# Two query tiles and two token tiles per step in a four-layer attention kernel

## The chip, the cores and the metric

The kernel runs on one core of a Trainium2 chip. The time is the device time of one execution in microseconds; the runs of the kernel before are summarised by their median. One further execution was recorded by the hardware profiler; its engine rows are the profile. The engines are PE (TensorE, matrix products into PSUM), ACT (ScalarE), DVE (VectorE), POOL (GpSimd) and SP (SyncE, which here only issues DMAs). PEld is the loading of a stationary operand into PE.

## The reference

The input is one sequence of 2048 tokens with 512 features, in bf16. Four residual layers follow each other: A, B, A, B, with the same weights for both A and both B:

```
x = x + A(layernorm(x));  x = x + B(layernorm(x));  and both once more

A: q, k, v = x wq, x wk, x wv           32 heads of 16, 4 segments of 512 tokens
   for each segment s:
     p      = softmax(q_s k_s^T / 4 + causal mask within the segment)
     a_dot  = p v_s
     a_mem  = phi(q_s) M / (phi(q_s) z + 1e-6)      phi(t) = t + 1 if t > 0 else exp(t)
     o_s    = g a_mem + (1 - g) a_dot               g = sigmoid(beta), per head
     M, z  += phi(k_s)^T v_s, sum of phi(k_s)
   return o wo

B: q, k, v = x wqkv;  pq, pk = q w_phi, k w_phi (16x16 per head)
   phi_q = [softmax(pq), softmax(-pq)], phi_k the same
   kv = phi_k^T v, z = sum of phi_k  over all 2048 tokens
   return (phi_q kv / (phi_q z + 1e-6)) wo
```

A works on segments of 512 tokens. B needs the sums over all tokens before its first query can be finished.

## The kernel before

Tokens are cut into 16 tiles of 128, four to a segment; heads into four groups of eight, a group being 128 of the 512 features. The residual X stays on chip for all four layers. `build` (L1035) runs through the layers L = 0 and 1 (each one A and one B): in A for each segment `a_proj` (K, Q, V and the memory sums), then `a_att` for each query tile, `out_proj` and the next layer's norm (`ln`) for each pair of tiles, then B's `b_keys` for the segment; after the fourth segment `b_query` for each of the four segments, in the first pass together with the norm and the projections of the second A.

Each function only writes down operations: an engine or a choice of engines, what it reads and writes, and which buffer it opens. The order of all operations is a written-out table (`ORDER`, L1106 on): `place` (L157) unpacks from it the order of the 3047 operations, the engine of each, and the buffer of each tile. `emit` hands each engine its operations in that order, with the waits on semaphores that the data and the reuse of buffers need. An engine thus never overtakes within its own list, SP and POOL neither.

The buffers that matter: PSUM is cut into four tiles D of 128 x 1024 fp32 (two banks each), used in turn for projections, scores, value products and outputs. `p1` are 20 buffers of 128 x 512, `p2` 18 of 128 x 1024, `pE` four for masked probabilities.

Where a matrix product has 64 rows, two of them run side by side, one in each half of PE's rows, and write the two banks of one D. `pair` (L330) splits a projection in that way into two operations of eight matmuls; both banks are complete after the second.

`a_att(L, s, i)` (L759) takes one query tile i of a segment. For each group of heads and each key tile j up to i it forms scores in a D (128 keys in rows, 1024 columns: eight heads by 128 queries) with eight matmuls of 128 columns (label S). On the diagonal, j = i, keys and queries are halved and the empty quarter is left out, 768 columns, and two matmuls with `two64` and `tri` add the mask (Sd). One ACT instruction takes the exponential (L351, 1024 elements a row, or 768 into a `pE` buffer). Then the value products (PV, L326): 16 matmuls of 34 columns for each key tile, probabilities stationary, values with a column of ones moving; all four groups of a tile collect in one D. When the four groups are there, DVE takes for each half of the heads the reciprocals (`rden`, 16 columns, L389) and the product (`pvn`, 256 elements, L834), adds the memory part (`oadd`, L842), and a DMA on SP (or PE for the last tile) transposes the tile for the output projection.

`out_proj` (L864) multiplies by wo for two tiles at once, but adds to X tile by tile: on DVE (`res`, 512 elements, L879), or, for certain tiles of B, X is added on PE and the sum evacuated (L359 on ACT or L360 on DVE). In the second B each tile is stored by its own DMA (issued through L368).

`a_proj` evacuates K, Q and V from PSUM by `evac`, on ACT (L359) or DVE (L360) as the table says, V tile by tile with 512 elements. `b_keys` (L903) projects keys and values for two tiles at once, but takes the exponentials (+ and -, L351) and their sums over 16 features (L925) tile by tile with 512 elements. Tiles 14 and 15 are projected singly.

## Time and profile before

| | |
|---|---|
| Runs of the kernel before | 494.85, 496.53, 498.26 us, median 496.53 |
| The profiled execution | 492.6 us, of which 490.9 us from the first to the last instruction (the span) |
| Instructions | 27,235: PE 12,490 matmuls and as many weight loads, DVE 1087, ACT 605, POOL 144 |
| Exponentials and other ACT work | 256 of 1024 elements, 128 of 768, 112 of 512, 55 evacuations, 54 small ones |
| Chain that ended last, by engine | PE 59%, ACT 25%, DVE 8%, issue 3%, DMA 3% |
| HBM read and written | 6.32 and 2.10 MB |

A group row names a line of the kernel, the engine, the operation, what it writes and reads, the shapes, and a count; then the busy time in us, the mean of one in ns, and the idle time ahead of the group with what ended it. Consecutive instructions of one engine overlap in these rows, the next begins before the last has left; a step is the distance of their starts. Line 326 is all of PE's work written by `mm`, 341 all written by `pair`, 351 all of ACT's written by `act`.

A row of the chain is the start in us, a length, and who was at work. A row of the windows is a stretch in us and its length; then for PE, PEld, DVE, ACT and POOL the busy time with the number of instructions; then the clock granted to PE as a share of the full one, the DMA engines' busy share and the GB/s. On the page each digit is the busy tenth of one of 40 slices of 12.3 us.

### The profile page before, as it was taken

Reading aid. Unit: us, or ns where it says so; the run is one execution under the profiler, and the core shown is the slowest. Engines: PE = TensorE matmul, PEld = TensorE weight load, DVE = VectorE, ACT = ScalarE, POOL = GpSimd, SP = SyncE. Lnnn points to the kernel's source line nnn. Section 1 sums busy time; section 2 is a strip of 40 time slices with the busy share of each in tenths; the row PEclk is TensorE's granted clock in tenths of the full one; section 3 lists DMA queues with packets and bytes.
Section 4 is the critical chain, followed back from the end, with each engine's and each line's share of the span. In section 5 each row is a group of like instructions: output and inputs, shape, how many; then the busy total and the mean of one; then the engine's idle time right before and its main releaser. Section 6 shows DMA issues by size and latency. Waiting matters only on the chain.

```text
span 490.9 us, 27235 instructions
## 1 busy us (share of the span) xinstructions
PE 460.2 (94%) x12490; PEld 309.1 (63%) x12490; DVE 436.1 (89%) x1087; ACT 433.9 (88%) x605; POOL 59.6 (12%) x144
## 2 busy tenths in 40 slices
PE   7899999999999989999999999899999999998896
PEld 3457666576667666665656766576577676665553
DVE  6899899899989969888999999899989997998884
ACT  3799899999999889579999999899999999858882
POOL 4701031010011001000230240100010010100000
PEclk9999999999999999999999999999999999999599
DMA  8761554441315021001124445153304133200255
GB/s 233 203 117 37 80 107 66 90 70 32 41 38 73 5 54 28 13 3 24 27 55 79 90 57 90 15 79 60 68 4 57 26 44 38 47 3 3 51 109 169
DMA packets 89459, 30.50 MB, mean 62 GB/s; under 512 B 76000, under 2 KB 89344, under 8 KB 89344
## 3 DMA queue, kind: packets, MB, share of 16 engines
q1 hardware_dynamic: 88992, 28.46, 31.7%
q8 instruction: 98, 1.61, 1.4%
q10 hardware_dynamic: 288, 0.26, 0.2%
q14 instruction: 17, 0.14, 0.1%
q0 software_dynamic: 64, 0.02, 0.1%
HBM read 6.32 MB, written 2.10 MB: 17 GB/s over the span
## 4 chain that ended last, share of the span: by engine, by line
PE 59%; ACT 25%; DVE 8%; issue 3%; DMA 3%; SPq 1%; POOL 0%; POOLq 0%; DVEq 0%
PE D L341 36%; PE D L326 21%; ACT p L351 16%; ACT pE L351 6%; DMA WA_q<-in_A_wq_dram 2%; DVE pQ L672 1%; ACT pS L351 1%; DVE p L756 1%; DVE pS L925 1%; PE D L854 1%; DVE pK L360 1%; ACT pV L359 1%; DVE p L591 1%; ACT p L359 1%; DVE p L360 1%
## 5 line engine op out<-in xcount | busy, mean ns | idle before, releaser
L351 ACT ACTIVATE p<-D 128x1024 bf16<-128x1024 f32 (+1 forms) x368 | 312.1, 913 | 25.2 <-PE D L326 11.6
L326 PE MATMUL D<-pK,pQ 64*128 64x128 bf16 (+1 forms) x2560 | 115.5, 211 | 4.3 <-ACT p L351 1.4
L326 PEld LDWEIGHTS D<-pK,pQ 64*128 64x128 bf16 x2560 | 80.7, 94 | 43.4 <-ACT p L351 10.9
L351 ACT ACTIVATE pE<-D 128x768 bf16<-128x768 f32 x128 | 102.0, 835 | 4.7 <-PE D L326 3.6
L326 PE MATMUL D<-pV,p 64*128 64x34 bf16 x1536 | 73.4, 176 | 3.9 <-issue 2.9
L326 PE MATMUL D<-pV,pE 64*128 64x34 bf16 x1024 | 75.2, 175 | 0.5 <-ACT pE L351 0.2
L326 PE MATMUL D<-pW,pE 64*128 64x34 bf16 x1024 | 73.0, 175 | 0.1
L326 PE MATMUL D<-pW,p 64*128 64x34 bf16 x1536 | 71.7, 176 | 1.0 <-issue 0.9
L326 PEld LDWEIGHTS D<-pV,p 64*128 64x128 bf16 x1536 | 66.8, 93 | 7.1 <-issue 2.4
L326 PEld LDWEIGHTS D<-pW,p 64*128 64x128 bf16 x1536 | 65.8, 93 | 3.9 <-issue 1.4
L341 PE MATMUL D<-pX,WA_k 64*128 64x512 bf16 x256 | 65.2, 376 | 2.1 <-DMA WA_q<-in_A_wq_dram 1.4
L341 PE MATMUL D<-pX,WA_q 64*128 64x512 bf16 x256 | 65.3, 377 | 0.6 <-issue 0.4
L578 POOL TENSOR_SCALAR rstd<-mv 128x1 f32<-128x1 f32 x60 | 14.9, 265 | 374.0 <-DVE mv L571 367.2
L326 PEld LDWEIGHTS D<-pV,pE 64*128 64x128 bf16 x1024 | 54.8, 93 | 3.1 <-issue 1.5
L326 PEld LDWEIGHTS D<-pW,pE 64*128 64x128 bf16 x1024 | 51.2, 93 | 0.9 <-issue 0.3
L570 DVE BATCH_NORM_STATS2 stats<-X 128x6 f32<-128x512 bf16 x64 | 42.5, 681 | 4.7 <-DMA X<-in_A_x_dram 4.6
L925 DVE TENSOR_REDUCE pS<-p 128x32 f32<-128x512 bf16 x64 | 42.1, 672 | 2.1 <-ACT p L351 1.9
L672 DVE TENSOR_SCALAR pQ<-p,m 128x512 bf16<-128x512 bf16 x128 | 42.6, 355 | 0.6 <-ACT p L359 0.5
L879 DVE TENSOR_TENSOR X<-X,D 128x512 bf16<-128x512 bf16 x48 | 31.1, 682 | 7.3 <-PE D L341 7.1
L580 POOL TENSOR_TENSOR rstd<-rstd,mhalf 128x1 f32<-128x1 f32 x60 | 36.4, 624 | 2.8
L341 PE MATMUL D<-WA_o,p 64*128 64x512 bf16 (+1 forms) x288 | 33.8, 353 | 2.3 <-issue 1.9
L326 PE MATMUL D<-tri,two 64*128 64x256 bf16 x256 | 35.2, 270 | 0.0
(117 smaller groups left out, 848.9 us busy)
## 6 DMA issues: line engine op xcount, KB each, us to landing
pW<-pV SPq DMA_DIRECT2D x16, 136.0 KB, 2.7
out_dram<-X SPq DMA_DIRECT2D x16, 128.0 KB, 1.9
X<-in_A_x_dram SPq DMA_DIRECT2D x3, 512.0 KB, 7.5
pX<-in_B_wqkv_dram SPq DMA_DIRECT2D x3, 512.0 KB, 5.4
p<-p SPq DMA_TRANSPOSE x76, 3.2
pX<-p SPq DMA_TRANSPOSE x54, 3.2
WA_k<-in_A_wk_dram SPq DMA_DIRECT2D x2, 256.0 KB, 6.7
WA_v<-in_A_wv_dram SPq DMA_DIRECT2D x1, 512.0 KB, 8.0
```

Of the source, the lines that this page charges most:

```text
L326: ins = e.matmul(out_ap, lhsT, rhs, start=st, stop=sp, tile_position=(basep(lhsT), basep(out_ap)))
L341: ins = e.matmul(out_ap, lhsT[64 * hf:64 * hf + 64], rhs[64 * hf:64 * hf + 64], start=k == 0 and i == 0, stop=k == 1 and i == len(lists[hf ...
L351: return self.g.op({"act": (dur, lambda e: e.activation(out_ap(), in_ap(), func, scale=scale))}, reads, writes, opens, label=label)
L359: ch = {"act": (n / 1.2 + 51, lambda e: e.activation(out_ap(), in_ap(), ACT.Copy)), "dve": ((340 if fast else n / 0.96 + 65), lambda e: e. ...
L360: "dve": ((340 if fast else n / 0.96 + 65), lambda e: e.tensor_copy(out_ap(), in_ap()))}
L570: v(lambda e: e.bn_stats(self.stats[:, t, :], self.X[:, t, :]), 602, [R("X", t)], [R("st", t)], label="bn")
L578: v(lambda e: e.tensor_scalar(rs, self.mv[:, t, 1:2], LN_EPS, None, op0=ALU.add), 170, [R("mv", t)], [R("rstd", t)], eng="pool", label="rstd")
L580: v(lambda e: e.tensor_tensor(rs, rs, self.mhalf[:], ALU.pow), 540, [R("rstd", t), R("mhalf")], [R("rstd", t)], eng="pool", label="rstd")
L591: v(lambda e: e.tensor_scalar(xn.t[:], self.X[:, t, :], self.mv[:, t, 0:1], self.rstd[:, t:t + 1], op0=ALU.subtract, op1=ALU.mult), 300, [ ...
L672: fn = lambda e, KM=KM, KT=KT, sl=sl: e.tensor_scalar(KM.t[:, :, sl % 2, :, 64 * (sl // 2):64 * (sl // 2) + 64], KT.t[:].rearrange("p (j h ...
L879: self.v(lambda e, X=X, src=src: e.tensor_tensor(X(), X(), src(), ALU.add), 602, [R("X", t), ps[512 * k]], [R("X", t)], label="res")
L925: fn = lambda e, sgn=sgn, E=E, Z=Z: e.tensor_reduce(Z.t[:, sgn * 32:(sgn + 1) * 32], E.t[:, sgn * 512:(sgn + 1) * 512].rearrange("p (h d) ...
```

## The change

Layer A takes two query tiles i0 and i0 + 1 together. Scores against the key tiles before them are formed for 256 queries and half of the heads of a group in a D (four matmuls of 256 columns). Against key tile i0 both query tiles have scores, and only the first one's are on the diagonal: a new form `Sf`, 896 elements a row, with its own buffers `pF`. Against key tile i0 + 1 only the second has, in the old diagonal form. Value products collect in a D for two groups of heads and both tiles, so that each reciprocal, product and addition works on half of the features of both tiles. That reorders the features of o, so the rows of wo are loaded in another order, in four DMAs instead of one, and the memory part is written in the new order too. o and its transpose are 128 x 1024 in `p2`.

Values are evacuated two tiles at a time, residual sums and stores too, and the exponentials of B's keys and their sums. `p1` has 16 buffers instead of 20, `p2` 19 instead of 18, `pE` two instead of four, `pF` three.

The table is new. It lists 2912 operations: PE 1054 (1022 before), ACT 566 (606), DVE 964 (1087), POOL 140 (140), SP 188 (192). Matmuls are not operations here; one operation of PE issues several.

```diff
-        ldw(lambda: self.WA["o"], inp["A_wo"], R("WA", "o"))
+        for kk in range(4):
+            load(lambda kk=kk: [(self.WA["o"][:, kk, :], inp["A_wo"].rearrange("(g k a x) o -> g a k x o", g=2, k=4, a=2)[kk // 2, kk % 2])], 128, [R("WA", "o", kk)])
...
-            for k in range(2):
-                self.evac(lambda tt=t2 + k: VT.t[:, tt, :, 0:16], ..., 512, [ps[k * 512]], [VT[t2 + k]], label="Vev")
+            self.evac(lambda t2=t2: VT.t[:, t2:t2 + 2, :, 0:16]..., 1024, [ps[0], ps[512]], [VT[t2], VT[t2 + 1]], label="Vev")
...
-    def a_att(self, L, s, i):
+    def a_att(self, L, s, i0):
...
+        for gg in range(2):
+            PV = self.T(self.pD, "pv")
+            for g in (2 * gg, 2 * gg + 1):
...
+                for j in range(i0 + 1):
+                    for p in range(2):
+                        S = self.T(self.pD, "S")
+                        if j < i0:
+                            P = PT[(p, j)] = self.T(self.p2, "PT")
+                            self.mm(lambda ...: [(S.t[:, hf * 512 + x * 256:hf * 512 + x * 256 + 256], key(hf, j, p, x), qry(hf, 0, 256), True, True)
+                                                 for x in range(2) for hf in range(2)], [], rd, [S], opens=[P], label="S", rows=64, dur=222)
+                            self.act(lambda P=P: P.t[:], lambda S=S: S.t[:], ACT.Exp, 1024, [S], [P], scale=0.25, label="exp")
+                        else:
+                            P = PF[p] = self.T(self.pF, "PF")
+                            self.mm(lambda ...: [
+                                (S.t[:, hf * 512 + 256 - 192 * x:hf * 512 + 512 - 256 * x], key(hf, j, p, x), qry(hf, 64 * x, 256 - 64 * x), x == 0, False)
+                                for x in range(2) for hf in range(2)] + [... two(hf), tri(hf, 2), False, True) for hf in range(2)],
+                                [], rd + trir, [S], opens=[P], label="Sf", rows=64, dur=252)
+                            self.act(lambda P=P: P.t[:, :, 64:512], lambda S=S: ...[:, :, 64:512], ACT.Exp, 896, [S], [P],
+                                     scale=0.25, label="expf")
...
+            v(lambda e, pvv=pvv, rden=rden: self.recip(e, rden(), pvv()[:, :, :, 16]), self.dur_recip(32), pvr, [Rt], label="rden")
+            v(lambda e, ...: e.tensor_tensor(part(o)..., pvv()[:, :, :, 0:16], rden()..., ALU.mult), 598, pvr + [Rt], [o[gg]], label="pvn")
+            if s >= 1:
+                v(lambda e, part=part: e.tensor_tensor(part(o), part(o), part(tmp), ALU.add), 335, [o[gg], tmp], [o[gg]], label="oadd", port=True)
...
+                self.tr(dst, lambda part=part: part(o), [o[gg]], [oT[gg]], [oT] if gg == 0 else [], label="otr")
...
-        for k, t in enumerate(ts):
...
+            self.v(lambda e: e.tensor_tensor(X(), X(), src(), ALU.add), 65 + 512 * n / 0.96, pr + xr, xr, label="res")
+        if store:
+            self.dma(lambda: [(self.out[0][t0 * 128:(t0 + n) * 128, :].rearrange("(t p) d -> p t d", p=128), self.X[:, t0:t0 + n, :])], 1, xr, [], lat=1900.0, label="store")
...
+                for sgn in range(2):
...
+                    self.act(..., ACT.Exp, 512 * n, [S[0], S[512]][:n], [E[sgn]], scale=1.0 - 2.0 * sgn, label="kexp")
...
+                    v(fn, 65 + 512 * n / 0.96, [E[sgn]], [Z[sgn]], label="Zred")
...
-                for i in range(4):
+                for i0 in (0, 2):
...
-N_XT, N_KM, N_K1, N_K2, N_VT, N_SM, N_QT, N_PE = 5, 6, 20, 18, 5, 6, 6, 4
+N_XT, N_KM, N_K1, N_K2, N_VT, N_SM, N_QT, N_PE, N_PF = 5, 6, 16, 19, 5, 6, 6, 2, 3
```

## The prediction

> **What bounds the kernel now.** I read the page's busy shares and slices first, then the chain of waits, then the groups by shape, then the timeline at the two ends.

> ```profile
> PE 460.2 (94%) x12490; PEld 309.1 (63%) x12490; DVE 436.1 (89%) x1087; ACT 433.9 (88%) x605; POOL 59.6 (12%) x144
> ...
> PE   7899999999999989999999999899999999998896
> ...
> DVE  6899899899989969888999999899989997998884
> ACT  3799899999999889579999999899999999858882
> ...
> PEclk9999999999999999999999999999999999999599
> ```

> Three engines are nearly full from slice 2 to slice 34; none alone is the limit. PE's 94% contains modelled ends: its columns, N/2.4 ns each with the two row halves side by side (a pair of 34-column value products starts every 25 ns in the timeline), come to 414 us, 84%. What keeps the others from 100% is mostly the start (ACT 3, 7) and the last five slices. In the two attention stretches, 40-200 and 217-425 us, the windows give ACT 347.8 us busy of 368, DVE 334.2, PE 349.8. Inside them the chain is ACT back to back, with PE's projections between:

> ```profile
> 362.57 0.92 ACT p L351
> 363.49 0.70 ACT pE L351
> 364.20 0.92 ACT p L351
> 365.11 0.70 ACT pE L351
> ...
> 373.92 0.50 ACT p L351
> ```

> These are the steps that one instruction really takes in a full queue: 1024 elements 0.917 us, 768 0.704, 512 0.49, so 0.833 ns per element and 0.063 fixed (the groups' means, 1043, 835 and 616 ns, contain the overlap with the next). DVE likewise, first in the timeline, then in the groups by shape:

> ```profile
> 265.45 1.29 DVE L360 CAST pV<-D 128x512 bf16<-128x512 f32 x2
> ```

> ```profile
> L925 DVE TENSOR_REDUCE pS<-p 128x32 f32<-128x512 bf16 x64 | 42.1, 672 | 2.1 <-ACT p L351 1.9
> L879 DVE TENSOR_TENSOR X<-X,D 128x512 bf16<-128x512 bf16 x48 | 31.1, 682 | 7.3 <-PE D L341 7.1
> ...
> L834 DVE TENSOR_TENSOR p<-D,pS 128x256 bf16<-128x256 f32 x64 | 25.3, 417 | 0.3
> ...
> L389 DVE RECIPROCAL pS<-D 128x16 f32<-128x16 f32 x64 | 13.4, 235 | 9.1 <-PE D L326 8.8
> ```

> Two casts in 1.29, one alone 0.69: a step of 0.60 for 512 elements, 0.533 for the elements and 0.067 fixed. So joining two operations saves 0.063 on ACT and 0.067 on DVE, and nothing else.

> **The change, engine by engine.** Assignments are those of the new order table, unpacked as the kernel unpacks it.

> PE. For one layer, segment and group, the scores were 6 full tiles (8 matmuls) and 4 diagonal ones (10), 88 matmuls; now 4 full (4), 4 half-masked (6), 2 diagonal (10): 60. Columns per row half: 6x512 + 4x640 = 5632 before, 4x512 + 4x576 + 2x640 = 5632 after. The same columns in half the matmuls stand side by side in the trace:

> ```profile
> 262.04 0.60 PE L341 MATMUL D<-WB_o,p 64*128 64x256 bf16 x8
> ...
> 262.48 0.61 PE L326 MATMUL D<-pK,pQ 64*128 64x128 bf16 x16
> ```

> 1024 columns a half take 0.60 as 8 and 0.61 as 16: at most 0.01 us for 8 matmuls fewer, so the 896 that go are worth 0 to -1.1 us. Value products stay at 5120, every projection stays. PE: 414.3 to 414.2.

> ACT. Score exponentials: 192x0.917 + 128x0.704 = 266.2; after, 128x0.917 + 128 of 896 elements + 64x0.704. No row has 896; between 768 and 1024 the ends are 0.704 and 0.917, which is 13.6 us either way over 128; the three measured sizes lie on a line within 10 ns, so I take 0.810 and get 266.2, no change, +-1.3. Key exponentials: 64x0.49 = 31.4 to 28x0.917 + 8x0.49 = 29.6 (-1.8). Value evacuations on ACT: 8x0.49 to 3x0.917 (-1.2). K and Q evacuations: 21 to 16 (-2.5). Weight folding: 3x0.49 + 1.07 to none (-2.5). Residual evacuations: 9x0.49 to 5x0.917 + 2x0.49 (+1.2). One each more of four small ones (+2.1). Sum -4.7: 419.6 to 414.9.

> [...]

> DVE. Products with the reciprocals: 64x0.334 to 32x0.60 (-2.2). Reciprocals: 64 of 16 columns to 32 of 32; the rows for 32 and 64 columns (334, 536 ns) give 6.3 ns a column, so each pair saves its fixed part, 0.03 to 0.067; I take 0.06 (-1.9). Key sums 64x0.60 to 28x1.133 + 8x0.60 (-1.9). Residual sums 48x0.60 to 22x1.133 + 4x0.60 (-1.5). Residual evacuations 7x0.60 to 1.133 + 2x0.60 (-1.9). Values 24x0.60 to 13x1.133 (+0.3). K, Q, folds, taken over from ACT (+5.4). Small ones -1.2. Sum -4.9: 422.4 to 417.5. The memory product keeps its 12x1024 elements in a longer pattern; L756 and L950, differently strided, both take 1.22, so 0. The 24 additions keep their size.

> Sums of 415-418 on three engines for a span of 491 mean that the order decides. The saved ACT time lies in the stretches where ACT is 94% busy; DVE has the same saving, so it does not become late in its place. PE is next: by columns it is 88% full there, and 4.7 us in 368 makes it 89%. Of the -4.7 I take -3.5; the ends are -5.6 (idle time shrinking in proportion, 4.7x491/415 = 5.6) and 0.

> **Start.** PE's first projection waits for weights:

> ```profile
> 3.30 8.56 DMA WA_q<-in_A_wq_dram
> ```

> Ahead of and with it went 2048 KB (four X tiles, half of wk, X 4-7, wv, half of wq). In the new table two of the four wo quarters (256 KB) stand second and fourth on SP, but wv and one half are behind: 1792 KB. At the 215 GB/s of the first 10 us, 256 KB are 1.2 us. Against it X tile 2 is issued one place later (0.5 us; PE's transposes end at 10.5 now, 1.4 before the weights). SP's seventh issue took 2.96 us in before, the others about half a microsecond; now the seventh is a weight half. Ends -1.2 and +1, taken -0.7.

> **End.** Sixteen stores become nine.

> ```profile
> 485.88 3.12 SPq L368 DMA_DIRECT2D out_dram<-X  x6
> ```

> The chain's last piece, a cast of 0.69 us at 486.39, gives the last result at 487.1, but SP still issues until 489.0, and landing takes 1.9. With pairs the queue is empty sooner; the last paired sum (1.13 instead of 0.60) takes part of it back. Ends -1.3 and 0, taken -0.8.

> **Waits and queues.** The two halves of a projected pair both end with its second set of eight matmuls, before and after, so a joined evacuation, exponential or residual sum waits for nothing new; it gives the first tile's half 0.53 us later (1.13 against 0.60), and behind it on DVE stands that tile's norm, 0.6 us a tile, whose consumer is a 3.2 us DMA. I cost this at 0 where other tiles' work is queued, which is everywhere but at the last pair. SP's transposes keep their number (110 of o and x, 28 others) and size. POOL has seven small memsets for six, and one of its four gate products is DVE's now (in the small ones above). A transposed half of o now holds both tiles, so the first tile of a pair waits for the second: rival 2.

> Sum: -3.5 - 0.7 - 0.8 = -5.0, from 492.6 to 487.6 in the profiled execution (span 490.9 and 1.7 around it). The three runs shown have a median of 496.5, so I put the forecast there: 491.5.

> **Rivals.**

> 1. The saving falls into idle time. In the list of waits ACT waits for PE 40 us in all, PE's weight loads for ACT 25; if the new order only widens these, the two ends remain: -1.5 at best, 495 to 497. For it: DVE and ACT save by almost the same amount while PE saves nothing. Against it: 94% ACT in 368 us.

> 2. The hand-over from A to B gets longer, and the kernel slower. Tiles 14 and 15 used to end one after the other, tile 14's projection, norm and transposing DMA (3.2 us) beneath tile 15's scores; now both end with the last pair. Summed by steps over the order, the work between the last value product of layer A and the first denominators of B grows from PE 18.1 and DVE 19.1 us to 26.0 and 28.6 in the second half of the kernel, and from 18.1 and 23.3 to 25.0 and 28.8 in the first, while ACT has 16 to 19. Cut at the last value product of each segment, at these points and where B of the first layer gives way to A of the second (its first scores, its last projection), the busiest engine's sums come to 436.0 before and 440.3 after: +4.3, in the ratio of 491 to 448 (the sum with 12 us of start) +4.7: 501, with start and end at nothing. It decides if the earlier stretches do not shorten by what moved: the first three segments go from 129.3 to 128.4 only.

> 3. The clock.

> ```profile
> 450.00:455.00 5.00, 3.30 (x194) 2.77 (x194) 3.35 (x12) 4.80 (x11) 0.00 (x0) 0.98 0.01 3
> 455.00:460.00 5.00, 3.50 (x136) 2.94 (x130) 4.26 (x10) 4.79 (x11) 0.00 (x0) 0.50 0.11 24
> 460.00:465.00 5.00, 4.82 (x54) 2.67 (x56) 3.81 (x10) 4.33 (x7) 0.00 (x0) 0.50 0.43 74
> ```

> PE, two thirds busy at 450-460, runs at 0.50 until 465: eight matmuls of a projection that take 1.04 took 1.89 at 460, about 3 us lost. The same place in the first half kept 1.00. If the longer hand-over leaves PE idle there too, +3; if the stretch goes, -3. [...] Alone: 494 to 500.

> **Numbers.** Forecast 0.48, rival 1 0.22, rival 2 0.22, rival 3 alone 0.08. A measurement of this kernel tells about 1% from no change: below 491.6 is faster, above 501.5 slower. Of the forecast's chance 0.38 lies below, rival 3's better side adds 0.02; rival 1 and the rest of the forecast are within; rival 2 and 3 together reach 504. Faster 0.40, same 0.34, slower 0.26. Range: below, -5.6 - 1.2 - 1.3 - 3 = -11.1, 485; above, +4.7 + 3 = +7.7, 504.

> **What would show it.** ACT near 429 us busy with 565 instructions, DVE near 431 with 964, PE's matmuls 11,594; the 896-element exponential at about 940 ns mean; first projection near 11.2; last result within 3 us of the end. Wrong would be: ACT under 90% in the attention stretches, more than 22 us between the last value product and the first denominators, or a second 5 in the clock's row.

## Result, and the profile after

The changed kernel takes 482.92 us (median; 481.20 to 483.33), the kernel before on the same chip 497.39 (494.85 to 498.28): a ratio of 0.971, 95% interval 0.967 to 0.976, some 14 us less. The forecast was 491.5. The profiled execution took 483.33 us with a span of 481.6. Medians, here and below, take in every execution of a kernel; ratios leave out those that took over 1.5% longer than its fastest.

The page of the kernel after, its engine sums and its slices:

```profile
PE 455.0 (94%) x11594; PEld 298.9 (62%) x11594; DVE 436.1 (91%) x964; ACT 426.9 (89%) x565; POOL 60.1 (12%) x144
...
PE   7889899989999999998999999999999989999896
...
DVE  4999999989899998988999999999999987998893
ACT  3499999999999997488999999999999999586992
...
PEclk9999999999999999998999999999999999999798
```

The counts are those of the prediction, and ACT lost 7.0 us of busy time. DVE lost 123 instructions and no busy time, PE 5.2 us. So the engines' work explains at most half of the 14 us. The groups by shape of the kernel after (busy time and mean, then the idle time ahead and what ended it):

```profile
L351 ACT ACTIVATE pF<-D 128x896 bf16<-128x896 f32 x128 | 117.6, 949 | 2.5 <-PE D L326 2.0
L942 DVE TENSOR_REDUCE pS<-p 128x64 f32<-128x1024 bf16 x28 | 33.4, 1208 | 1.6 <-ACT p L351 1.6
L895 DVE TENSOR_TENSOR X<-X,D 128x1024 bf16<-128x1024 bf16 x22 | 26.7, 1219 | 7.6 <-PE D L341 7.2
L844 DVE TENSOR_TENSOR p<-D,pS 128x512 bf16<-128x512 f32 x32 | 21.9, 685 | 0.5
L389 DVE RECIPROCAL pS<-D 128x32 f32<-128x32 f32 x32 | 11.3, 353 | 2.4 <-PE D L326 2.1
```

The joined forms cost what was worked out. What is new stands in the last column: DVE's reciprocals waited 9.1 us for PE's value products before and wait 2.4 now. PE became earlier there, though it has the same columns to multiply. The rest of the study is about why.

**A place where PE stands still.** Two rows of the groups of before were there to be read and were not:

```profile
L326 PE MATMUL D<-pV,p 64*128 64x34 bf16 x1536 | 73.4, 176 | 3.9 <-issue 2.9
...
L326 PE MATMUL D<-pW,p 64*128 64x34 bf16 x1536 | 71.7, 176 | 1.0 <-issue 0.9
```

"Issue" is idle time that no semaphore ended. These matmuls lie inside an operation of 16; what the operation waits for, its first matmul has waited for. To find where the idle time lies, PE's recorded instructions (a weight load, a matmul and a recorded wait each count as one) were numbered from the first, and the idle time was sorted by the number modulo 256, in 64 places of four. One place stands out: 192 to 195, with 7.2 of the 25.1 us that PE is idle in the kernel before. The other 63 places have about 0.3 us each. The queue q8, which carries instructions, counts blocks of the same size. Before:

```profile
q8 instruction: 98, 1.61, 1.4%
```

After:

```profile
q8 instruction: 91, 1.49, 1.3%
```

```profile
PE D L326 <- issue: 8.6, 15, 1.2
...
PE D L341 <- issue: 2.5, 4, 1.0
```

The kernel after:

```profile
PE D L341 <- issue: 1.3, 1, 1.3
...
PE D L326 <- issue: 1.0, 3, 0.5
```

All kernels of the study, "place" being PE's idle time at the border, in us, in the profiled execution. Ratios are against the kernel before on the same chip:

```
kernel                          median  ratio [95%]            span   place  matmuls
before, first profile           497.39  -                      490.9   7.2   12,490
before, profiled again          499.63  -                      497.8  13.1   12,490
  same order, token joins       501.63  1.004 [1.000, 1.008]   499.6  11.6   12,490
  +64 small matmuls             507.64  1.020 [1.012, 1.028]   504.2  18.0   12,554
  +128                          500.21  0.999 [0.995, 1.002]   498.6  11.3   12,618
  value products, full rows     501.38  1.002 [0.999, 1.006]   500.4   1.2    9,930
after                           482.92  0.971 [0.967, 0.976]   481.6   1.4   11,594
  +32 small matmuls             493.06  0.985 [0.982, 0.989]   490.9  11.0   11,626
  +64                           500.32  1.001 [0.997, 1.005]   498.6  16.1   11,658
  +128                          483.78  0.967 [0.964, 0.971]   482.0   1.1   11,722
  full scores in 128 columns    496.16  0.994 [0.990, 0.998]   496.3  14.0   12,106
  all scores in 128 columns     503.46  1.008 [1.005, 1.012]   502.9  19.8   12,618
  value products, full rows     496.65  0.996 [0.992, 0.999]   495.0   1.5    9,034
  token joins undone            487.30  0.974 [0.968, 0.980]   485.2   1.6   11,594
  division joins undone         488.07  0.976 [0.970, 0.981]   485.8   1.8   11,594
  all joins undone              492.28  0.985 [0.982, 0.988]   489.5   2.0   11,594
  other load order              483.10  0.968 [0.961, 0.976]   484.3   2.6   11,594
  load order, 173 cuts          482.50  0.963 [0.961, 0.966]   481.7   2.0   11,767
  2048 instructions of waits    562.55  1.129 [1.122, 1.135]   563.3   6.9   11,594
```

### The profile page after: what moved, and what is told of

The parts are those of the page before. It is cut to its first block, busy times and chain, and to the rows that moved or that the text cites. A ratio compares the mean times of both kernels' runs of the same rounds, so it can differ in the third digit from the quotient of the medians.

```text
span 481.6 us, 25267 instructions
## 1 busy us (share of the span) xinstructions
PE 455.0 (94%) x11594; PEld 298.9 (62%) x11594; DVE 436.1 (91%) x964; ACT 426.9 (89%) x565; POOL 60.1 (12%) x144
## 4 chain that ended last, share of the span: by engine, by line
PE 59%; ACT 26%; DVE 7%; DMA 3%; issue 2%; POOL 1%; SPq 0%; DVEq 0%
PE D L341 38%; PE D L326 20%; ACT p L351 13%; ACT pF L351 9%; ACT pE L351 3%; DMA p<-p 2%; DVE pQ L676 1%; DMA X<-in_A_x_dram 1%; DVE stats L574 1%; POOL rstd L584 1%; ACT pS L351 1%; PE D L864 1%; DVE p L595 1%; DVE X L895 1%; DVE p L761 1%
## 5 line engine op out<-in xcount | busy, mean ns | idle before, releaser
L351 ACT ACTIVATE p<-D 128x1024 bf16<-128x1024 f32 (+1 forms) x276 | 251.6, 964 | 27.2 <-PE D L341 19.5
L326 PE MATMUL D<-pK,pQ 64*128 64x256 bf16 (+3 forms) x1536 | 114.8, 243 | 7.1 <-ACT p L351 2.3
L351 ACT ACTIVATE pF<-D 128x896 bf16<-128x896 f32 x128 | 117.6, 949 | 2.5 <-PE D L326 2.0
L326 PEld LDWEIGHTS D<-pK,pQ 64*128 64x128 bf16 x1536 | 54.7, 94 | 45.7 <-ACT pF L351 6.9
L326 PE MATMUL D<-pV,pF 64*128 64x34 bf16 x1024 | 76.4, 176 | 2.4 <-ACT pF L351 1.1
L326 PE MATMUL D<-pW,pF 64*128 64x34 bf16 x1024 | 74.3, 176 | 0.0
L341 PE MATMUL D<-pX,WA_k 64*128 64x512 bf16 x256 | 64.7, 376 | 0.9 <-ACT pX L359 0.8
L341 PE MATMUL D<-pX,WA_q 64*128 64x512 bf16 x256 | 64.7, 377 | 0.0
L326 PEld LDWEIGHTS D<-pV,pF 64*128 64x128 bf16 x1024 | 56.9, 93 | 5.7 <-ACT pF L351 2.3
L351 ACT ACTIVATE pE<-D 128x768 bf16<-128x768 f32 x64 | 53.1, 839 | 1.8 <-PE D L326 1.2
L326 PEld LDWEIGHTS D<-pW,pF 64*128 64x128 bf16 x1024 | 53.5, 93 | 1.1
L326 PE MATMUL D<-pV,p 64*128 64x34 bf16 x1024 | 52.2, 176 | 0.1
L326 PE MATMUL D<-pW,p 64*128 64x34 bf16 x1024 | 51.3, 176 | 0.0
L326 PEld LDWEIGHTS D<-pV,p 64*128 64x128 bf16 x1024 | 46.8, 93 | 2.5 <-ACT pF L351 0.4
L326 PEld LDWEIGHTS D<-pW,p 64*128 64x128 bf16 x1024 | 45.5, 93 | 1.5
L326 PE MATMUL D<-tri,two 64*128 64x128 bf16 (+1 forms) x384 | 45.9, 234 | 0.0
L326 PE MATMUL D<-pV,pE 64*128 64x34 bf16 x512 | 44.7, 175 | 0.0
L326 PE MATMUL D<-pW,pE 64*128 64x34 bf16 x512 | 42.9, 175 | 0.4 <-issue 0.2
L942 DVE TENSOR_REDUCE pS<-p 128x64 f32<-128x1024 bf16 (+1 forms) x36 | 38.3, 1086 | 1.6 <-ACT p L351 1.6
```

Of the source, the lines that this page charges most:

```text
L326: ins = e.matmul(out_ap, lhsT, rhs, start=st, stop=sp, tile_position=(basep(lhsT), basep(out_ap)))
L341: ins = e.matmul(out_ap, lhsT[64 * hf:64 * hf + 64], rhs[64 * hf:64 * hf + 64], start=k == 0 and i == 0, stop=k == 1 and i == len(lists[hf ...
L351: return self.g.op({"act": (dur, lambda e: e.activation(out_ap(), in_ap(), func, scale=scale))}, reads, writes, opens, label=label)
L942: fn = lambda e, sgn=sgn, eo=eo, Z=Z, n=n: e.tensor_reduce(Z.t[:, 0:64 * n].rearrange("p (k s h) -> p k s h", k=n, s=2)[:, :, sgn, :], eo( ...
```

## Experiments

**First group: joins against PE's program.** If the time came from fewer and larger instructions on DVE and ACT, undoing joins must give it back. If it came from PE's fewer matmuls, the same columns in more matmuls must. The token joins (values, residual sums, stores, key exponentials and sums) undone, the order and PE's program kept:

```diff
-            self.evac(lambda t2=t2: VT.t[:, t2:t2 + 2, :, 0:16]..., 1024, [ps[0], ps[512]], [VT[t2], VT[t2 + 1]], label="Vev")
+            for k in range(2):
+                self.evac(lambda tt=t2 + k: VT.t[:, tt, :, 0:16], ..., 512, [ps[k * 512]], [VT[t2 + k]], label="Vev")
...
-            self.v(lambda e: e.tensor_tensor(X(), X(), src(), ALU.add), 65 + 512 * n / 0.96, pr + xr, xr, label="res")
+            for k, t in enumerate(ts):
+                self.v(lambda e, X=X, src=src: e.tensor_tensor(X(), X(), src(), ALU.add), 602, ..., label="res")
```

> The kernel after, in its own order and buffers, with the token-tile joins undone in place: each value evacuation, residual sum or evacuation, key exponential, key sum and store that covers two tiles becomes two, one right behind the other on the same engine. That adds 36 instructions to ACT and 65 to DVE: 36 x 0.063 = 2.3 us and 65 x 0.067 = 4.4 us of steps. Three theories of the 14.5 us between the two medians. (A) Fixed parts: the gain is the fixed parts of the joined instructions, each paid once at about the price of its step; then this kernel takes 2.3 to 4.4 us more than the kernel after. (B) Hand-overs: every joined instruction also removes a wait between engines, which costs a multiple of the step; then 7 us more or above. (C) Attention form: the gain comes from scoring and multiplying two query tiles together and from the order of that work; then 0 to 1.5 us more.

The reciprocals and products with them by halves:

```diff
-            v(lambda e, ...: self.recip(e, rden(), pvv()[:, :, :, 16]), self.dur_recip(32), pvr, [Rt], label="rden")
+            for a in range(2):
+                v(lambda e, ..., a=a: self.recip(e, rden(a), pvv()[:, a, :, 16]), self.dur_recip(16), pvr, [Rt[a]], label="rden")
```

> The kernel after, in its own order and buffers, with the 32 reciprocals of 32 columns and the 32 products of 512 elements cut into halves again, 64 and 64, neighbours on the same engine. Steps added on DVE: 32 x 0.067 for the products and 32 x 0.06 for the reciprocals, 4.1 us. (A) Fixed parts: 2 to 4 us more than the kernel after. (B) Hand-overs: 7 us more or above, since PE waits for the buffer of the value products that these instructions hold. (C) Attention form and order: 0 to 1.5 us more.

The other way round, the token joins put into the kernel before, in its own order:

> The kernel before, with its own attention, its own order and buffers, and only the token-tile joins of the change: values, key exponentials and key sums, residuals and stores for two tiles, each at the place of the earlier of the two instructions that it replaces. 35 instructions fewer on ACT, 65 on DVE: 2.2 and 4.4 us of steps. (A) Fixed parts: 2.2 to 4.4 us less than the kernel before. (B) Hand-overs: 7 us less or more than that. (C) Attention form and order: 0 to 1.5 us less, and up to 2 us more where a joined instruction gives the first tile's half later in an order that was not made for it.

And the scores of the kernel after in matmuls of at most 128 columns, as before had them; every column stays (the full scores are shown, the half-masked ones are cut likewise):

```diff
-  [(S.t[:, hf * 512 + x * 256:hf * 512 + x * 256 + 256], key(hf, j, p, x), qry(hf, 0, 256), True, True)
-   for x in range(2) for hf in range(2)]
+  [(S.t[:, hf * 512 + x * 256 + c:hf * 512 + x * 256 + c + 128], key(hf, j, p, x), qry(hf, c, 128), True, True)
+   for x in range(2) for c in (0, 128) for hf in range(2)]
```

> The kernel after with its full and half-masked scores written again by matmuls of at most 128 columns: 1024 more matmuls and weight loads (896 fewer was the change), the same columns, the same order. My price from the rows (1024 columns a half take 0.60 us as 8 matmuls and 0.61 as 16): 0 to 1.3 us more than the kernel after. Against it stands the theory that PE's weight loads or its fetching of instructions are a limit that the profile hides in busy time and in the 'issue' of its chain: then 4 us more or above.

Undone token joins gave 487.30, undone division joins 488.07: a part of the gain each, and most of it stayed. The joins in the order of before gave no gain (1.004): DVE's busy time fell by 4.5 us against before's second profile, and its idle time, the span less the busy time, rose from 60.7 to 67.0. The 1024 further matmuls took all of it back and more: 503.46, 1.008 of the time before. In the steady rows of the trace more matmuls at the same columns cost next to nothing (0.61 us for 16, 0.60 for 8), so the prediction's price for them was wrong by some 20 us. The list of waits of this kernel names it:

```profile
PE D L326 <- issue: 12.6, 16, 1.8
PE D L341 <- issue: 5.7, 6, 1.7
```

and its windows show two borders in a row (the stretch and its length, then busy time and instructions of PE, PEld, DVE, ACT, POOL; granted clock, DMA share, GB/s):

```profile
89.80:92.40 2.60, 2.58 (x141) 2.35 (x134) 2.34 (x5) 2.51 (x4) 0.84 (x2) 1.00 0.36 55
92.40:93.36 0.96, 0.01 (x1) 0.00 (x1) 0.96 (x4) 0.46 (x1) 0.00 (x0) 1.00 0.05 5
93.36:96.29 2.93, 2.58 (x128) 2.27 (x128) 2.63 (x5) 2.60 (x4) 0.00 (x0) 1.00 0.74 93
96.29:97.36 1.07, 0.00 (x2) 0.00 (x1) 0.00 (x0) 0.64 (x1) 0.00 (x0) 1.00 0.25 43
```

PE works, stops for 0.96 us, works through exactly 128 matmuls and 128 loads, and stops for 1.07, at the full clock. The packets of q8 lie at 90.53-91.94 and 95.08-96.04: PE goes on 1.4 and 1.3 us after each has landed, and the second begins 1.7 us after PE went on. Over the stops longer than 0.3 us in the eight traces that have most of them, a fetch starts some 1.2 us (1.0 to 1.9 in nine of ten) after PE goes on behind a border, takes 1.1 us (0.9 to 1.4), and PE goes on 1.4 us (1.3 to 1.6) after it landed. If a block's crossing starts the fetch of the next one, and PE cannot go on without it, a block lasts about 3.7 us at least, by adding up these three. In the trace of before a pair of 34-column value products starts every 25 ns, of 128-column scores every 56 ns, of 512-column projections every 216 ns; at these steps 64 pairs, a block, would be done in 1.6, 3.6 and 13.8 us. The theory from here on: **PE's program comes one block ahead, and PE waits where a block of small matmuls is done before the next one is there.** The rival: each matmul has a price of its own.

**Second group: where the borders fall.** The kernel before itself was profiled again; PE of the kernel after was given waits that are always fulfilled (2048 instructions with no matmul); the loads of its start were reordered (below); and 64 matmuls of 34 columns were put among before's warm-up matmuls (products of ones at the start, before any data has come), which moves every border by half a block:

```diff
+                    for _ in range(64):
+                        e.matmul(D.t[:, 0:34], self.onesb[:], self.onesb[:, 0:34], start=True, stop=True, tile_position=(0, 0))
```

> The kernel before, unchanged, profiled once more. What is asked: 1024 more matmuls at the same columns (scores of 128) took 20.5 us, and in that profile PE stands idle 19.8 us at one place of its program, each time 256 instructions on (a matmul and its weight load are two), against 1.4 us in the kernel after and 7.2 us in the 492.6 us execution of before. (D) Instruction supply: PE waits for the next 256 instructions of its program wherever it uses them up faster than they come. Then a second execution of before has its idle time at the same place of the 256, and more of it than 7.2 us if it is slower than 492.6: the part of its time that varies is there. (W) Weight loads in the array are what the smaller matmuls cost: then nothing is special about that place, and it has about 0.4 us as every other of the 64 places that I divide the 256 into.

> The kernel after with 2048 instructions more in PE's program that move no data: eight waits on a semaphore that has long been reached, ahead of each full and half-masked score operation, as many instructions as the 128-column scores added there. (D) Instruction supply: as dear as those, 12 to 25 us, and the idle time of PE again at one place of each 256 instructions. (W) Weight loads or the array: nothing of either is added, 0 to 2 us. If it costs time, but spread over all places of the 256, the sequencer's own time for a wait is the cause, and this run tells nothing.

> The kernel before with 64 small matmuls more among PE's first ones, before any data has come: 128 instructions, half of 256, so that every later place where 256 instructions are used up lies 64 matmuls earlier in the work; nothing else changes. (D) Instruction supply: the idle time stays at the same place of the 256, so it falls on other work, its sum 4 to 13 us; the time is that of before, up to 5 us more or less. (W) The idle time belongs to the work (scores that wait for ACT or a buffer): its place among the 256 moves by 128.

Before's two profiles differ by 6.9 us of span and 5.9 us at the place, with the same program: most of the difference between these two executions is idle time at the place. The 64 matmuls at the start, worth under 2 us themselves at 25 ns each, made the kernel 10 us slower (507.64 against 497.61; up to 5 had been expected), and the idle time at the place rose to 18.0 us.

The waits settle nothing:

```diff
+            for _ in range(16 if label in ("S", "Sf") else 0):
+                e.wait_ge(self.g.esem["dve"], 1)
```

By the author's count two of these waits make one instruction, eight an operation, 2048 in all. The kernel took 562.55 us, 80 us more than after, but the idle time is spread over all places (74.6 us in all, 6.9 at the border). Where such instructions follow one another in this trace they start 106 ns apart, and PE had half the clock for 59 us of this execution (mean granted clock 0.949), against 15 in after (0.987); both hide what the run was made to show.

**Third group: the rows of the value products, and the borders of after.** In full rows a value product takes half as many matmuls of the same 34 columns, each with 128 rows instead of a pair of 64. (It leaves out keeping apart the two heads of a pair, so the attention values are other numbers; the matmuls, evacuations and transposes are those of a kernel of this form.)

```diff
-                                for ab in range(2):
-                                    rows = slice(64 * ab, 64 * ab + 64)
...
+                                V = VT.t[:, j].rearrange("p (a k) c -> p k a c", a=2)[:, k]
+                                r.append((PV.t[:, c:c + 34], P, V, j == 0 and x == 0, j == i0 + ii and x == 1))
```

In the kernel before, and in the one after:

> The kernel before with half the matmuls in its value products: one matmul on all 128 rows in place of two on 64 rows each, 2560 for 5120, so 5120 instructions of PE fewer in 25,110. What is left out: the two heads that share a tile of probabilities are not kept apart, each output is the sum of both, so the result is not the reference's; every exponential, product, reciprocal, DMA, wait and buffer stays. PE's time for them stays too: among the first matmuls of the trace those of 128 rows and 34 columns start every 25 ns, as the pairs of 64 rows do in the value products. (D) Instruction supply: the idle time at the one place, 13.1 us in the last profile of before, goes nearly all: 8 to 13 us less than before, 485 to 490. (W) Weight loads or columns of the array: 0 to 2 us less.

> The kernel after with the same halving of the value products (the same part left out: two heads are not kept apart). (D) Instruction supply: only 1.4 to 2.6 us stood at the one place in after and in the kernel with another load order, so 1 to 3 us less than the kernel after, 480 to 482. More than 6 us less would mean that the number of PE's instructions costs time at other places too, and (D) in this form is too narrow.

The 64 matmuls in the warm-up of after, and only its full scores (not the half-masked `Sf`) cut to 128 columns, 512 matmuls more:

> The kernel after with 64 small matmuls more among PE's first ones, the shift by half of 256 instructions that cost before 10 us. (D) with fewer instructions as the reason: PE uses 256 instructions up more slowly now wherever the places fall, 0 to 3 us more than the kernel after and under 5 us at the one place. (D) with luck as the reason: the new order happens to have its places where PE is slow anyway; then 5 us more or above, and 7 us or more at the one place.

> The kernel after with only its full scores written by matmuls of 128 columns, and the half-masked ones left as they are: 512 matmuls more in place of 1024, which took 20.5 us. (D) Instruction supply: 5 to 12 us more than the kernel after, in the last two segments of each layer half above all, 4 to 10 us at the one place of the 256. (W) 0 to 1 us more.

The shift alone turned after into a kernel as slow as before: 500.32, ratio 1.001. Its timeline of PE at two borders (start, length, what; in brackets the idle time before):

```profile
94.93 0.20 PE L326 MATMUL D<-pW,pF 64*128 64x34 bf16 x2
96.12 0.17 PE L326 MATMUL D<-pV,pF 64*128 64x34 bf16 x1 [0.99 <-issue]
...
100.03 0.17 PE L326 MATMUL D<-pW,p 64*128 64x34 bf16 x1
102.43 0.18 PE L326 MATMUL D<-pW,p 64*128 64x34 bf16 x1 [2.23 <-issue]
```

One partner of a side-by-side pair comes 2.4 us after the other: nothing of the data can explain that. And the list of waits:

```profile
PE D L326 <- issue: 14.5, 17, 2.2
...
PE D L341 <- issue: 1.5, 3, 0.7
```

Cutting only the full scores gave 496.16, ratio 0.994, with 14.0 us at the place. The full rows left 1.2 and 1.5 us of idle time at the place, but both kernels were slower than had been expected: 501.38 where 485 to 490, and 496.65 where 480 to 482 stood. The page of the kernel after with full rows shows one reason:

```profile
PE 473.6 (96%) x9034; PEld 298.2 (60%) x9034; DVE 437.9 (88%) x964; ACT 432.5 (87%) x565; POOL 60.1 (12%) x144
```

PE is busy 18.6 us longer with 2560 matmuls fewer. Between a matmul of 64 rows and one of 128 the trace has a longer step than between two of a kind: by 85 ns behind a value product and by 94 to 95 ns elsewhere, at the transposes of before too (308 ns instead of 213 behind a 512-column matmul, 148 instead of 53 behind one of 128). Before has 49 such changes and after 47, the two kernels with full rows 321 and 329, some 275 more, worth about 25 us. The pairs' 25 ns held. The comparison of these two kernels is still of use: neither loses at the place, and the change is worth 4.7 us there (501.38 to 496.65, on one chip).

**Fourth group: whole blocks, a quarter block, all joins.** If the place decides and not the added matmuls, 128 of them, a whole block, must cost nothing, while 32 must cost. The first ten warm-up matmuls are cut to 34 columns there so that the start is not longer:

```diff
-            unit(128, 512, 1)
+            unit(128, 512 if k >= 10 else 34, 1)
...
+                    for _ in range(128):
+                        e.matmul(D.t[:, 0:34], ...)
```

> The kernel after with 128 small matmuls more among PE's first ones, 256 instructions, and ten of the first 512-column matmuls cut to 34 columns so that the start stays as long. The places where 256 instructions are used up fall on the same work as in after; 64 matmuls more had cost 17 us. (P) Place: what counts is where in the work the blocks of 256 end; then 481 to 486, and under 3 us idle at the one place. (M) The added matmuls themselves do the harm, at the start or through the clock: then 497 or more, as with 64.

> The kernel before with the same 128 matmuls more; 64 had cost 10 us. (P) Place: the time of before again, 495 to 501, with 7 to 13 us idle at the one place. (M) Added matmuls: 507 or more.

> The kernel after with 32 small matmuls more, a quarter of 256 instructions. If every block of 256 instructions that PE gets through in under 3.5 us costs what is missing to 3.5, the blocks of the profile of after, cut anew, cost 2.9 us as they stand, 10.4 with 32 matmuls more and 13.9 with 64 (1.4 and 16.1 were found in the profiles). So (P) Place: 8 to 12 us idle at the one place and 488 to 494 us in all; (M) a time that only depends on whether matmuls were added: 497 to 503.

> The kernel after with all joined instructions split at once (values, key exponentials and sums, residuals, stores, reciprocals and products); PE's program and its places are unchanged. One by one they cost 4.4 and 5.2 us. If they add up: 491 to 494, and the joins are 8 to 11 us of the gain of 14.5. If one hides the other: 487 to 490.

A whole block costs nothing in either kernel (0.967 and 0.999), a quarter costs 9 us (493.06 against 483.78), a half 15 to 17 (the ratio 1.001 against 0.971 and 0.967). More matmuls, less time: the rival with a price for each is out. After, shifted by a whole block, in the list of waits:

```profile
PE D L326 <- issue: 0.5, 2, 0.3
...
PE D L341 <- issue: 0.4, 1, 0.4
```

All joins undone, with PE's program unchanged, gave 492.28, on the same chip as the 483.78 of the shifted after: 8.5 us for the joins together. The page of this kernel:

```profile
PE 460.3 (94%) x11594; PEld 298.7 (61%) x11594; DVE 446.6 (91%) x1092; ACT 430.4 (88%) x601; POOL 60.5 (12%) x144
```

DVE has 128 instructions and 10.5 us more, ACT 36 and 3.5. So once PE does not wait for its program, most of DVE's fixed parts count; in the order of before, with 11.6 us lost at the place, the token joins bought nothing.

**The start, and a version that avoids the borders.** Of the loads at the start, X tile 2 stands behind quarters of wo in the new table. Put ahead of them:

```diff
+        first = [0, 2, 4, 5, 7, 6, 11, 10, 13, 15]
+        at = sorted(k for k, o in enumerate(order) if o.id in first)
+        for k, i in zip(at, first):
+            order[k] = self.ops[i]
```

> The kernel after with the first ten loads on SP in another order: X tiles 0 and 2, wk and wq (first halves, then second), X tiles 4 to 7, wv, and the two quarters of wo last, which stood second and fourth. The first projection stood at 13.8 us in after and 11.9 in before, and in after DVE waits 3.4 us for X tile 2 behind a quarter of wo. If the start counts in full, the first projection comes at 11 to 11.9 and the kernel takes 2 to 3 us less than the kernel after. If the saving falls into a later wait (wv comes 256 KB earlier, X 4 to 7 256 KB later), 0 to 1 us less.

The first projection came at 12.9 us instead of 13.8, the lead was 0.6 to 1.1 us until 279 and was lost behind that, and the time stayed: 483.10.

Last, that load order together with 173 matmuls of 512 columns in projections cut in two, chosen so that the borders fall into projections rather than value products:

```diff
+SPLITS = {134: 2, 795: 1, 1261: 7, 1262: 8, ...}
...
+                            cut = 2 if 2 * i + hf < SPLITS.get(box[k].id, 0) else 1
+                            for c in range(cut):
+                                half = lambda a: a[:, a.shape[1] // cut * c:a.shape[1] // cut * (c + 1)]
```

> The kernel after with the load order of the seventh experiment and 173 of its 512-column matmuls cut into two of 256 columns (346 instructions of PE more, the same columns), chosen so that the blocks of 256 instructions end in projections: by the block durations of after the sum of what is missing to 3.4 us falls from 2.2 to 0.6. (P) Place: no loss from the added matmuls, and at most 1 to 2 us less than the kernel after, 481 to 483, with under 1 us at the one place. If the number of matmuls were what costs, 173 more would cost 3 to 4 us (1024 cost 20.5): 486 to 487.

482.50 us, ratio 0.963 [0.961, 0.966]: the 173 matmuls cost nothing, and nothing is shown to be gained over after, which loses only 1.4 us at the place to begin with. The choice of borders missed its own aim: 2.0 us at the place, where under 1 was expected.

## Why the prediction was wrong, step by step

**The step that failed** is PE's: "the 896 that go are worth 0 to -1.1 us". The row it rests on holds (0.60 for 8 matmuls, 0.61 for 16), and in the trace of before the step of a pair grows by 0.417 ns a column, the N/2.4 ns that had been taken (56 ns at 128 columns, 216 at 512); at 34 columns it is 25 ns. But the wait for the program's next block was not in the sum: it was put at nothing without being named. At 25 ns a pair a block of value products is done in 1.6 us, against the 3.7 estimated above for the next one to be there. The idle time at the place was 7.2 and 13.1 us in the two profiles of before and is 1.4 in after.

What that is worth: within after's order the spans rise by 9.3 us for 9.6 at the place (32 added) and by 17.0 for 14.7 (64 added), within before's by 6.9 for 5.9, so 1.0 to 1.2 us for each. Applied to pairs of executions:

```
before -> after                    span    of it at the place   rest
first profile -> after             -9.3    -5.8 to -7.0         -2.3 to -3.5
profiled again -> after           -16.2   -11.7 to -14.0        -2.2 to -4.5
both with 128 more                -16.6   -10.2 to -12.2        -4.4 to -6.4
both with 64 more                  -5.6    -1.9 to -2.3         -3.3 to -3.7
both with full rows                -5.4    +0.3 to +0.4         -5.7 to -5.8
```

So the order and the work gave 2 to 6 us, and the forecast of 5.0 for them lies in that; the program's supply gave another 6 to 14, for which the forecast had 0 to 1.1. That the 5.0 fits is partly luck. Start and end, 1.5 of it, brought nothing (below), while all joins together were worth 8.5 us, where 3.5 had been taken for the engines' saving; so something else in the new form and order cost some us. The later start and the longer hand-overs are candidates, and no run separates them. The **transfer to the median** failed with PE's step: the 4 us between the profiled execution of before and its median were carried over as if after had them too. Before's second profile, 497.8 us with 13.1 at the place, suggests that they were this idle time, which after does not have; the other executions have no profile.

**Is it fewer matmuls, or where the borders happen to fall?** Both kernels have a good cut. An estimate from the traces, adding up what each block lacks to 3.5 us (the author's choice, near the 3.7 above), for 16 positions of the borders, gives 7.8 to 21.8 us for before, mean 16.8, its own position being the lowest; for after 2.9 to 16.5, mean 10.1, again its own the lowest. By that some 5 to 7 us go with the program of after, wherever the borders fall. The traces of the two kernels with scores in 128 columns tell what of it is the number of matmuls, since they have after's order: the same estimate gives a mean of 13.3 us with 512 matmuls more and 16.7 with 1024 more, which is before's. The estimate is rough: at a kernel's own borders it is up to 5 us off what its profile has. The shift runs show that the borders' position alone can take the whole gain; the split between number and position remains an estimate.

**The mechanism** is shown as far as the place and its price go: a whole block more costs nothing, half a block costs the whole gain. That the place is the border of two fetched blocks, and that the fetch begins only when a border is crossed, one block ahead, is read from the numbers and times of q8's packets (98 and 91, each of 16 KB) and was not tested by a run of its own. In these runs the crossings cost up to 19.8 us in a kernel (all scores in 128 columns) and up to 2.2 us at one border (shifted after), as PE gets through 256 instructions in 2.93 us (the third window above). PE stops behind a single fast block, as the fourth window shows; how much of its program PE holds was not measured.

The other steps:

- **ACT**: 426.9 us with 565 instructions, forecast about 429 and 565. The 896-element exponential has a mean of 949 ns against 940, and a step of 0.798 in a full queue against 0.810; 1024 take 0.904 and 512 take 0.477.
- **DVE**: 964 instructions as forecast, 436.1 us instead of 431. Counted from start to start, products with the reciprocals, key sums, residual sums, residual evacuations and reciprocals saved 2.3, 1.7, 1.3, 2.0 and 0.9 us (forecast 2.2, 1.9, 1.5, 1.9 and 1.9). What ACT handed over cost some 4 (forecast 5.4), but the norm's sums 1.5 and a gate product 1.4, where the small ones were to bring 1.2.
- **Start**, forecast -0.7: wrong. The timeline of after has the first projection at 13.79 us, 11.9 before, and the wait before it ends with ACT, not with weights:

```profile
13.79 0.37 PE L341 MATMUL D<-pX,WA_k 64*128 64x512 bf16 x1 [0.78 <-ACT pX L359]
```

The late X tile 2, priced at 0.5 us with 1.4 of room, kept DVE waiting for 3.4 us. The order of loads gave 0.9 back at that point and nothing at the end.
- **End**, forecast -0.8: nothing came of it. From the last projection to the end of the last store's issue it is 1.8 us instead of 2.6, but a store of two tiles takes a median of 3.2 us to land instead of 1.9, and from the last projection to the last landing it is 4.1 us instead of 4.0.
- **Rival 1** (the saving falls into idle time) did not come in after's order: ACT's idle time in the two attention stretches fell from 9.1 to 3.8 us and from 8.1 to 3.0. In before's order with the joins alone, it is what happened: DVE's idle time rose by more than its busy time fell.
- **Rival 2** (a longer hand-over from A to B) was right in its sums and in its own sign ("more than 22 us"): 19.5 to 26.6 us in the first half, 19.9 to 28.7 in the second. Its price was wrong because of the stretches that it was weighed against, where "129.3 to 128.4 only" had been expected of three segments: from the last value product of segment 0 to that of segment 3 it took 131.0 and 128.1 us before (133.0 and 127.9 in the second profile) and 122.6 and 115.2 after. The program's supply explains little of that: of before's 7.2 us at the place 3.8 lie in these stretches, 7.5 of the 13.1 in the second profile, none in the hand-overs. With full rows, where neither kernel loses at the place, the stretches are still shorter by 5.6 and 11.1 us and the hand-overs longer by 7.0 and 8.8. So the stretches lost about what the hand-overs gained; why the sums did not have it stays open.
- **Rival 3** (the clock) made no difference in sum: 14.2 us at half clock before, 14.8 after. The stretch at half clock is there again, in the windows of after:

```profile
445.00:450.00 5.00, 4.06 (x156) 3.03 (x150) 4.49 (x13) 4.97 (x11) 0.00 (x0) 0.50 0.01 3
450.00:455.00 5.00, 4.03 (x58) 1.86 (x56) 4.16 (x11) 3.85 (x6) 0.00 (x0) 0.82 0.54 68
```

The clock column, third from the end, has 0.50 and 0.82 there, some 7 us at half clock; before it had 0.50 from 455 to 465, some 10. Whether PE's idle time brings the half clock on, as this rival took it, no run shows. The 8 in the clock's row of after, near 225 us, is a second stretch of some 3 us that before does not have, behind the first hand-over, where this rival had looked for one.

## What to carry to other kernels

Price PE's program too, not only its columns: count its instructions in blocks of 256, as the packets of these runs have them. In these traces PE stopped behind blocks of small matmuls, whatever the data did: 1.07 us behind one that took 2.93, and 2.2 us even behind one of 4.1 with 16 matmuls of 512 columns in it (shifted after, 96.1 to 100.2), so the 3.7 us remain an estimate. "Issue" as the releaser of idle time inside one operation is the sign, and a shift of the whole program by half a block, a few small matmuls at the start, shows in one run how much hangs on it; compare kernels that differ in their matmul count only with that in mind. Ask of a saving on DVE or ACT whether it falls into a wait: the token joins bought nothing in one order, where PE lost 11.6 us at the borders, and all joins together 8.5 us in the other, where it lost 1 to 2. Whether the borders or the order, which was not made for the joins, kept the first from counting is not shown.

## What the runs showed of the hardware that was not expected

- The supply of PE's program: packets of 16 KB, 98 for 25,110 instructions before and 91 for 23,314 after; at the stops over 0.3 us of eight traces a fetch of about 1.1 us that starts about 1.2 us after PE has gone on behind a border, and 1.4 us until PE goes on again; up to 2.2 us lost at one border (shifted after).
- A change between matmuls of 64 and of 128 rows cost 85 to 95 ns in the traces of before and of the two kernels with full rows: 148 ns instead of 53 behind a 128-column matmul, 308 instead of 213 behind one of 512 (before).
- Waits on PE that were long fulfilled were not free: one behind another they started 106 ns apart, and 2048 instructions of them made the kernel 80 us longer (562.55 against 482.92), 59 us of it at half clock.
- A whole block of 128 matmuls more at the start cost nothing that shows (a ratio of 0.967 to before, 0.971 without them), a quarter of one 9 us (493.06 against 483.78).
